# A hand-ordered attention and expert kernel: one key load moved behind the weights, two factor products and a weight conversion re-seated, four stores issued by ScalarE

## The chip, the cores and the metric

The kernel runs on one core of a Trainium2 chip. The metric is the device time of one execution in microseconds (us): a median of 152.86 us over three runs (152.83 to 153.1). Five engines share the work, each with its own instruction list that it works off strictly in order: TensorE (PE in the profile), VectorE (DVE), ScalarE (ACT), GpSimd (POOL) and SyncE (SP), which issues most of the transfers. A wait in one list holds everything behind it on that engine.

## The reference

Two stages follow each other. The first is attention with 4 batches, 8 heads, 768 tokens and head size 64. A query sees the 8 first ("global") keys and a window of 96 keys behind it, with a bias that falls with distance, a slope per head:

```
scores = scale * q @ k.T
keep = is_global | is_local          # first 8 keys, or 0 <= i-j < 96
scores = where(keep, scores + bias, -1e9)
a = exp(scores - max); a = a / (sum(a) + 1e-9)
attn = a @ v
```

The second takes the 3072 tokens of 512 numbers that result:

```
h = x @ w_in                          # 512 -> 1024
solu = h * softmax(h)
ln = (solu - mean) / sqrt(var + 1e-6) * g_ln
out = ln @ w_out                      # 1024 -> 512
```

## The kernel before

**Tiling.** Heads are worked on in pairs (4 pairs per batch). The scores of a pair are cut into two groups of key blocks (queries 0 to 383 need the first, the rest the second too). The second stage goes by 24 tiles of 128 tokens. Batch 0 is on the critical path at the start; from about 26 us on, the second stage of one batch is interleaved with the attention of the next.

**Attention, step by step.** A pair's k or q is loaded as fp32 (`x32_`, lines 477 and 484), converted to fp16 (`x16_`, helper lines 264 on ScalarE, 266 on VectorE, 268 on GpSimd), turned by six TensorE transposes into a bank of PSUM (line 741), and copied out of the bank as `kT` or `qT`. In the last batch the turn is a DMA transpose (776). TensorE forms the scores (878 and 892), ScalarE their exponential `eb` (900). In batches 1 to 3 the bias is not added but multiplied in afterwards, as a factor `fb` (909, "the factor product"): on VectorE in one instruction, on GpSimd in four pieces. TensorE then sums the weights (973, 982), spreads the logarithm of the sums (1028), ScalarE takes the reciprocal `rr` (1037), and TensorE multiplies by v in two halves (1072); between the halves VectorE copies one number out of the bank (`tick`, 1082), and the second half waits for it. VectorE makes the product `xT` (1097), which is the input of the second stage.

**Second stage.** First product with w_in (1133), exponential `ef` (1140), `uu` (1143), its squares (1150 or 1154), a turn of `uu` (by TensorE at 1169, or by DMA at 1159), the second product (1215), a scaling into `osb` (1226, 1229) and the store (1233). Before the second product can run, w_out is loaded, multiplied by g (644, 647, 651: "weighing"), its mean taken on TensorE (658) and subtracted by eight VectorE instructions (662: "the centring").

**What sets the order.** All steps are numbered while the program is written; nothing else decides their order than the table `ORDER`, a list of these numbers, from which the five instruction lists follow. `SLOTS` gives each step its buffers, among them the eight PSUM banks; `ENGS` gives the engine of a step that has a choice; `WARM` places matmuls without use among the first steps. Transfers issued by SyncE and ScalarE take turns over eight semaphores, so that each issue waits until the transfer eight before it has landed.

Of the kernel before, what the change touches and what calls it, by code (L numbers as in the profile page):

```python
# [60 lines left out]
"""  # L61
SLOTS = """
# [10 lines left out]
"""  # L73
ENGS = """
# [1206 lines left out]
```

## Time and profile before

| | |
|---|---|
| Median of three runs | 152.86 us |
| The profiled execution | 152.65 us, of it 150.9 us span of instructions |
| TensorE busy | 142.4 us (94%) |
| ScalarE / VectorE / GpSimd busy | 122.1 / 117.9 / 69.9 us |
| Granted TensorE clock | full in all 40 slices |
| DMA busy | 9 tenths or more in 30 of 40 slices |

The page gives each engine's busy time, the busy tenths in 40 slices and the chain of work that ended last, followed back from the end. The timeline lists instructions with their start in us from the span's start, their length, and in square brackets the idle time of the engine just before them with what ended it; neighbours of one form are merged into a row (x4 is four instructions, and the length is that from the first start to the last end). Instructions of an engine overlap by some 0.05 to 0.08 us when they follow each other without a hole. PEld is TensorE's loading of weights, which comes just ahead of the matmul.

### The profile page before, as it was taken

How to read it: one execution, taken by the hardware profiler on the slowest of the kernel's cores; microseconds unless marked ns; L12 is line 12 of the kernel's file. 1: busy time of each engine (PE TensorE's matmuls, PEld its weight loads, DVE VectorE, ACT ScalarE, POOL GpSimd, SP SyncE). 2: the span in 40 equal slices, each digit the busy share in tenths (PEclk: the TensorE clock that was granted, in tenths of full speed). 3: DMA queues.
4: the chain of work that ended last, by engine and by line, in shares of the span. 5: the costliest groups of instructions: out<-in, count | busy, mean ns of one | idle time of the engine just before them, and what ended most of it. 6: DMA issues, size and time to landing. Idle time of an engine off the chain costs nothing.

```text
span 150.9 us, 4802 instructions
## 1 busy us (share of the span) xinstructions
PE 142.4 (94%) x1870; PEld 76.7 (51%) x1870; DVE 117.9 (78%) x241; ACT 122.1 (81%) x209; POOL 69.9 (46%) x192
## 2 busy tenths in 40 slices
PE   5979799999998999999999999999999999999991
PEld 2536556466554566744454645444446644444450
DVE  6939897998999997989899966697785874898200
ACT  3949899899999789899997987978895776874641
POOL 6784447559899769735922240498130000110000
PEclk9999999999999999999999999999999999999999
DMA  4999999999999999999999999998999946488743
GB/s 140 367 307 342 300 382 337 362 337 401 309 295 182 247 323 220 240 216 250 241 160 235 260 161 260 162 221 159 223 212 260 216 125 128 81 245 208 231 152 139
DMA packets 76430, 36.35 MB, mean 241 GB/s; under 512 B 65456, under 2 KB 71928, under 8 KB 76408
## 3 DMA queue, kind: packets, MB, share of 16 engines
q1 hardware_dynamic: 76120, 35.54, 97.5%
q10 hardware_dynamic: 288, 0.52, 0.9%
q8 instruction: 14, 0.23, 0.6%
q14 instruction: 8, 0.07, 0.1%
HBM read 23.15 MB, written 6.29 MB: 195 GB/s over the span
## 4 chain that ended last, share of the span: by engine, by line
PE 72%; ACT 9%; DMA 7%; SPq 5%; DVE 4%; issue 1%; DVEq 0%; ACTq 0%
PE acc L1215 28%; PE acc L1133 23%; PE acc L1072 6%; DMA vt<-in_v_dram 4%; DMA x<-in_q_dram 3%; PE acc L892 3%; ACT eb L900 3%; PE acc L1028 3%; PE acc L973 2%; PE acc L741 2%; SPq L477 2%; ACT ef L1140 2%; DVE x L266 2%; PE acc L1062 1%; SPq L499 1%
## 5 line engine op out<-in xcount | busy, mean ns | idle before, releaser
L1215 PE MATMUL acc<-gw_out_sb,late 128*128 128x512 f16 (+1 forms) x200 | 44.3, 371 | 0.4 <-DMA vt<-in_v_dram 0.4
L1133 PE MATMUL acc<-w_in_sb,xT 128*128 128x512 f16 x192 | 44.7, 379 | 0.0
L1143 DVE SCALAR_TENSOR_TENSOR uu<-ef,acc 128x1024 f16<-128x1024 f16 x24 | 29.2, 1216 | 8.6 <-ACT ef L1140 8.4
L900 ACT ACTIVATE eb<-acc 128x896 f16<-128x896 f32 (+1 forms) x32 | 29.1, 955 | 1.5 <-PE acc L892 1.4
L1140 ACT ACTIVATE ef<-acc 128x1024 f16<-128x1024 f32 x24 | 24.7, 1030 | 6.5 <-PE acc L1133 6.5
L1215 PEld LDWEIGHTS <-late 128*128 128x128 f16 x200 | 18.9, 98 | 21.5 <-issue 1.3
L1133 PEld LDWEIGHTS <-xT 128*128 128x128 f16 x192 | 17.8, 98 | 21.4 <-issue 1.4
L268 POOL CAST x<-x 128x384 f16<-128x384 f32 (+1 forms) x32 | 17.9, 586 | 12.3 <-DMA x<-in_q_dram 6.2
L1097 DVE TENSOR_TENSOR xT<-acc,rr 128x384 f16<-128x384 f32 x32 | 16.3, 551 | 3.9 <-ACT rr L1037 1.5
L1072 PE MATMUL acc<-eb,v 64*64 64x160 f16 (+4 forms) x448 | 16.0, 221 | 0.6 <-DVE xT L1097 0.3
L1150 ACT ACTIVATE sqa<-uu 128x1024 f16<-128x1024 f16 x15 | 15.9, 1063 | 0.0
L909 POOL TENSOR_TENSOR eb<-eb,fb 128x240 f16<-128x240 f16 (+1 forms) x20 | 12.5, 656 | 6.1 <-ACT eb L900 6.1
L1072 PEld LDWEIGHTS <-v 64*64 64x64 f16 x448 | 12.9, 106 | 4.5 <-issue 3.4
L1037 ACT ACTIVATE rr<-acc 128x768 f32<-128x768 f32 x16 | 12.6, 811 | 2.8 <-PE acc L1028 1.9
L268 POOL CAST v<-v 128x384 f16<-128x384 f32 (+3 forms) x23 | 10.9, 492 | 7.2 <-DMA v<-in_v_dram 6.3
L909 DVE TENSOR_TENSOR eb<-eb,fb 128x896 f16<-128x896 f16 (+1 forms) x19 | 13.3, 727 | 1.1 <-ACT eb L900 1.1
L741 PE MATMUL acc<-ident,x 128*128 128x128 f16 x144 | 11.1, 220 | 1.5 <-ACT x L264 1.0
L892 PE MATMUL acc<-qT,kT 64*64 64x160 f16 (+2 forms) x384 | 11.8, 227 | 0.0
L1154 DVE SCALAR_TENSOR_TENSOR sqv<-uu 128x1024 f16<-128x1024 f16 x9 | 11.3, 1251 | 0.1
L741 PEld LDWEIGHTS <-x 128*128 128x128 f16 x144 | 8.5, 98 | 4.8 <-ACT x L264 1.4
L1226 ACT ACTIVATE x<-acc,rstd 128x512 f32<-128x512 f32 (+1 forms) x9 | 5.8, 640 | 6.2 <-PE acc L1215 6.2
L1062 PE MATMUL acc<-eg,vgz 64*64 64x384 f16 x64 | 10.7, 324 | 0.0
(120 smaller groups left out, 206.1 us busy)
## 6 DMA issues: line engine op xcount, KB each, us to landing
x<-in_q_dram SPq DMA_DIRECT2D x16, 384.0 KB, 5.8
x<-in_k_dram SPq DMA_DIRECT2D x16, 384.0 KB, 5.1
out_dram<-osb SPq DMA_DIRECT2D x12, 256.0 KB, 4.9
v<-in_v_dram SPq DMA_DIRECT2D x12, 192.0 KB, 4.5
out_dram<-x SPq DMA_DIRECT2D x9, 256.0 KB, 2.3
late<-in_moe_w_in_dram SPq DMA_DIRECT2D x4, 512.0 KB, 6.6
w_out<-in_moe_w_out_dram SPq DMA_DIRECT2D x4, 512.0 KB, 6.0
v<-in_v_dram SPq DMA_DIRECT2D x12, 160.0 KB, 4.7
```

The lines of the kernel that those rows point to most:

```text
L268: nc.gpsimd.tensor_copy(out=out, in_=in_)
L741: nc.tensor.transpose(out=pt[:, ts(j, P)], in_=a[:, j, ts(pp, P)], identity=ident)
L892: nc.tensor.matmul(out=sc[o : o + 64, par, col : col + n], lhsT=kk[r, BLK * c : BLK * c + BLK], rhs=qq[r, g0 : g0 + n], start=fresh, stop= ...
L900: ex["fn"] = (lambda ex=ex, qk=qk, gw=gw: nc.scalar.activation(out=eb[at(qk, "eb")][:, :, 0:gw], in_=big(qk)[:, :, 0:gw], func=AF.Exp, sca ...
L909: (nc.gpsimd if fx["at"] == "POOL" else nc.vector).tensor_tensor(out=e[:, :, y], in0=e[:, :, y], in1=fb[:, p, :, y], op=ALU.mult)
L1072: nc.tensor.matmul(out=o_[64 * h : 64 * h + 64, gl : gl + m], lhsT=vv[r, v_at(vi, h, c), pair, :], rhs=view(eb[at(e_own[b, gi, pair], "eb" ...
L1097: nc.vector.tensor_tensor(out=xT[at(xt_own[b], "xT")][:, p, q0:q1], in0=one(av, d)[:, 0:w], in1=rr[at(re, "rr")][:, d, 0:w], op=ALU.mult)
L1133: nc.tensor.matmul(out=ph()[:, ts(fh, 512)], lhsT=xT[at(xt_own[b], "xT")][:, j, ts(t % NA, P)], rhs=w_in_sb[:, j, ts(fh, 512)], start=((j, ...
L1140: ex["fn"] = lambda g1=g1, t=t, ph=ph: nc.scalar.activation(out=ef[at(g1, "ef")], in_=ph(), func=AF.Exp, accum_out=s0[:, t : t + 1])
L1143: u["fn"] = lambda u=u, g1=g1, t=t, ph=ph: nc.vector.scalar_tensor_tensor(out=uu[at(u, "uu")], in0=ef[at(g1, "ef")], scalar=USC, in1=ph(), ...
L1150: nc.scalar.activation(out=sqs_["ACT"], in_=uu[at(u, "uu")], func=AF.Square, scale=float(D_FF) ** 0.5, accum_out=s2[:, t : t + 1])
L1215: nc.tensor.matmul(out=one(g2)[:, 0:wd], lhsT=uT[at(el_o, "uT")][:, c, :], rhs=gw_out_sb[:, c, sl_], start=(c == 0), stop=(c == NFC - 1))
```

## The change

- The load of the k of pair 1 of the second batch (`x32_3`) stands behind the third and fourth quarter of w_in and the load of g on SyncE. Its turn on TensorE stands behind the first two tiles of the first product, and goes to bank 7 and not 2. ScalarE copies it out behind the second `ef`.
- One of the casts of w_in (second half of its first quarter) goes from ScalarE to GpSimd.
- The turn of the last q of batch 0 goes to bank 0 and not 4.
- The eight small memsets of `slr` go from GpSimd to VectorE.
- The factor product of the second group of pair 0, batch 1 (`eb9`), goes from VectorE to GpSimd; that of pair 1 (`eb10`) stays on VectorE but stands behind the centring.
- Four stores of tiles below 20 go from SyncE to ScalarE. Some GpSimd steps near 96 to 103 us change places.

```diff
 ORDER = """
-126 86 12 11 271 2 13 17 16 10 15 66 14 18 0 20 73 36 3 75 7 1 4 88 68 69 89 22 53 55 56 90 8 70 38 79 81
+126 271 2 52 86 12 11 18 66 13 73 0 36 3 53 17 20 7 16 38 10 15 14 1 79 4 88 28 68 115 22 60 75 117 69 89
...
 WARM = """
-25:0:16 30:2:4 37:3:2 48:5:3 118:7:4
+34:0:16 43:2:4 49:3:2 59:5:3 126:7:4
...
     def constants_slr():
         for h in range(H):
-            nc.gpsimd.memset(slr[:, h : h + 1], -slopes[h] * NL)
+            nc.vector.memset(slr[:, h : h + 1], -slopes[h] * NL)
...
-    slr_st = step("POOL", 270, -59000, [], constants_slr, name="c_slr")
+    slr_st = step("DVE", 560, -59000, [], constants_slr, name="c_slr")
...
-                        wd * 1.31, tg + 2500, [ou], eng=("SP",) if x < 20 else ("SP", "ACT"), name="store", iss=420)
+                        wd * 1.31, tg + 2500, [ou], eng=("SP", "ACT"), name="store", iss=420)
```

GpSimd's list between 21 and 35 us of the trace, as a difference (x32_3 is the moved k, x32_5 the q of pair 3, x32_0 and x32_1 the k of pairs 2 and 3, all of the second batch; kg holds the global keys):

```order
 L268 CAST v16_1_115<-v32_0_111 128x2x3x64
+L268 CAST w_in_sb_69<-late_154 128x512 x4
 L268 CAST x16_3_110<-x32_3_103 128x384 x2
-L268 CAST w_in_sb_69<-late_154 128x512 x3
-L523 TENSOR_TENSOR kg1_127<-kT1_117,hpick_84 128x16
 L268 CAST x16_2_109<-x32_4_104 128x384 x2
 L268 CAST x16_0_107<-x32_5_105 128x384 x2
+L909 TENSOR_TENSOR eb9_139<-eb9_139,fb_166 128x2x112 x4
 L647 TENSOR_TENSOR gw_out_sb_71<-w_out32_70,g32_72 128x256 x2
 L268 CAST x16_3_110<-x32_0_100 128x384 x2
+L523 TENSOR_TENSOR kg1_127<-kT1_117,hpick_84 128x16
 L268 CAST x16_2_109<-x32_1_101 128x384 x2
```

Four pieces of a factor product and one kg product now stand ahead of the conversion of x32_1, and four casts of w_in ahead of that of x32_3.

VectorE's list from 39 to 50 us of the trace, before:

```order
L909 TENSOR_TENSOR eb11_141<-eb11_141,fb_166 128x960
L909 TENSOR_TENSOR eb10_140<-eb10_140,fb_166 128x2x448
L1097 TENSOR_TENSOR xT0_98<-acc_158,rr1_147 128x384
L266 COPY late_154<-acc_158 128x1024
L1097 TENSOR_TENSOR xT0_98<-acc_158,rr1_147 128x384
L662 SCALAR_TENSOR_TENSOR gw_out_sb_71<-w_out32_70,g32_72,acc_158 128x512 x8
L1143 SCALAR_TENSOR_TENSOR uu3_153,sums3_92<-ef1_149,acc_158 128x1024
L266 COPY qT0_121<-acc_158 128x768
```

and in the changed kernel:

```order
L909 TENSOR_TENSOR eb11_141<-eb11_141,fb_166 128x960
L1097 TENSOR_TENSOR xT0_98<-acc_158,rr1_147 128x384
L266 COPY late_154<-acc_158 128x1024
L1097 TENSOR_TENSOR xT0_98<-acc_158,rr1_147 128x384
L662 SCALAR_TENSOR_TENSOR gw_out_sb_71<-w_out32_70,g32_72,acc_158 128x512 x8
L1143 SCALAR_TENSOR_TENSOR uu3_153,sums3_92<-ef1_149,acc_158 128x1024
L909 TENSOR_TENSOR eb10_140<-eb10_140,fb_166 128x2x448
L266 COPY qT0_121<-acc_158 128x768
```

The product of eb10 moved behind the eight centring instructions and one `uu`; the set of instructions in this stretch is the same.

## Rows read from the trace of the kernel before

**Rows 1.** The page: the chain that ended last, shares by engine.

```profile
PE 72%; ACT 9%; DMA 7%; SPq 5%; DVE 4%; issue 1%; DVEq 0%; ACTq 0%
```

**Rows 2.** The chain in order of time: start us, us, what.

```profile
48.17 1.89 PE acc L1215 x8
...
56.36 0.30 PE acc L1072 x5
```

**Rows 3.** Busy us by stretch: PE, PEld, DVE, ACT, POOL, clock, DMA share, GB/s.

```profile
38.95:56.20 17.25, 16.70 (x225) 8.81 (x222) 17.25 (x29) 15.71 (x28) 14.05 (x29) 1.00 1.09 264
...
57.00:147.80 90.80, 90.76 (x1050) 46.51 (x1047) 67.75 (x129) 71.61 (x128) 29.11 (x68) 1.00 0.97 202
```

**Rows 4.** Timeline of VectorE: start us, us, engine, instruction [idle before].

```profile
35.30 0.96 DVE L266 COPY kT<-acc 128x768 f16<-128x768 f16 x1
36.30 0.16 DVE L1082 COPY tick<-acc 128x1 f32<-128x1 f32 x1
...
37.19 1.02 DVE L1097 TENSOR_TENSOR xT<-acc,rr 128x384 f16<-128x384 f32 x2 [0.32 <-PE acc L892]
...
38.88 0.16 DVE L1082 COPY tick<-acc 128x1 f32<-128x1 f32 x1
...
56.16 0.14 DVE L1082 COPY tick<-acc 128x1 f32<-128x1 f32 x1
```

**Rows 5.** Timeline of TensorE and its weight loads around 34.5 us.

```profile
34.42 0.77 PE L741 MATMUL acc<-ident,x 128*128 128x128 f16 x6
...
34.85 0.17 PEld L741 LDWEIGHTS <-x 128*128 128x128 f16 x3 [0.26 <-POOL x L268]
```

**Rows 6.** Timeline of GpSimd, 27 to 35 us.

```profile
27.38 0.21 POOL L523 TENSOR_TENSOR kg<-kT,hpick 128x16 f16<-128x16 f16 x1 [1.13 <-ACT kT L264]
...
28.90 0.96 POOL L268 CAST x<-x 128x384 f16<-128x384 f32 x2 [0.41 <-DMA x<-in_q_dram]
31.66 1.18 POOL L647 TENSOR_TENSOR gw_out_sb<-w_out,g 128x256 f16<-128x256 f32 x2 [1.80 <-DMA w_out<-in_moe_w_out_dram]
32.78 2.01 POOL L268 CAST x<-x 128x384 f16<-128x384 f32 x4
```

**Rows 7.** Timeline of GpSimd: its factor products elsewhere.

```profile
96.54 2.31 POOL L909 TENSOR_TENSOR eb<-eb,fb 128x224 f16<-128x224 f16 x4 [5.89 <-ACT eb L900]
...
58.52 2.74 POOL L909 TENSOR_TENSOR eb<-eb,fb 128x240 f16<-128x240 f16 x4
...
41.66 4.81 POOL L909 TENSOR_TENSOR eb<-eb,fb 128x240 f16<-128x240 f16 x8
```

**Rows 8.** Timeline of VectorE: a factor product, and two conversions of q or k.

```profile
28.04 0.92 DVE L909 TENSOR_TENSOR eb<-eb,fb 128x896 f16<-128x896 f16 x1
...
30.26 0.56 DVE L266 CAST x<-x 128x768 f16<-128x768 f32 x1 [0.15 <-DMA x<-in_q_dram]
...
59.70 1.06 DVE L266 CAST x<-x 128x768 f16<-128x768 f32 x1
```

**Rows 9.** Timeline of ScalarE at 17.7 us and TensorE at 25.4 us.

```profile
17.74 0.58 ACT L959 ACTIVATE eg<-acc,gbias 128x384 f16<-128x384 f32 x1 [0.38 <-PE acc L946]
...
25.42 0.51 PE L741 MATMUL acc<-ident,x 128*128 128x128 f16 x6
25.77 0.60 PE L1133 MATMUL acc<-w_in_sb,xT 128*128 128x512 f16 x2
```

**Rows 10.** Timeline of VectorE and of GpSimd around 11 us.

```profile
11.01 0.72 DVE L266 CAST x<-x 128x768 f16<-128x768 f32 x1 [2.55 <-DMA x<-in_q_dram]
...
10.99 0.33 POOL L374 MEMSET slr<- 128x1 f32 x8
```

**Rows 11.** Timeline of ScalarE at 82.7 us, and a store it issues late.

```profile
82.68 0.81 ACT L1037 ACTIVATE rr<-acc 128x768 f32<-128x768 f32 x1 [0.77 <-PE acc L1028]
...
143.37 0.37 ACTq L1233 DMA_DIRECT2D out_dram<-x  x1
```

**Rows 12.** Timeline of TensorE at 48.2 us.

```profile
48.17 0.38 PE L1215 MATMUL acc<-gw_out_sb,late 128*128 128x512 f16 x1 [0.43 <-DMA vt<-in_v_dram]
```

82 rows, old and new, of tables (ENGS, ORDER, SLOTS) are left out of this document.

## The prediction, as put on record before the run

> **What bounds the kernel now.** I read the chain that ended last first, since it says where a gain would count. TensorE holds 72% of it [rows 1], and from 48 us on it is TensorE alone [rows 2]. The table by stretch says the same of the end: from 57 to 147.8 us TensorE is busy for 90.76 of 90.8 us [rows 3]. So whatever TensorE has lost or won by 57 us is lost or won at the end; nothing behind it can be hidden or recovered but a few tenths.
>
> What sets the time at 57 us? At 56.36 the second half of an attention product starts [rows 2], and the VectorE copy it waits for (`tick`) runs from 56.16 to 56.30 [rows 4]: 0.06 us from one to the other. TensorE waits for VectorE there. And VectorE is busy for 17.25 of the 17.25 us from 38.95 to 56.20 [rows 3]: one run of 29 instructions without a hole. The start of this run sets its end.
>
> Followed backwards, the run begins behind the tick at 38.88. That waits for an attention product, whose bank is freed by the `xT` products at 37.19, which wait for TensorE (0.32 idle); that work waits for the tick at 36.30; and this stands behind the copy of `kT` at 35.30 [rows 4]. The copy needs six transposes of k that start at 34.42 and stop halfway: the last three begin at 34.85, and what TensorE waited for is GpSimd's conversion [rows 5]. GpSimd converts in two pieces, and the second of this k ends at 34.79 (32.78 + 2.01) [rows 6]. So one conversion on GpSimd, of the k of pair 3 of batch 1, carries the time of the whole kernel through five engine hand-overs. GpSimd is the least busy engine of all, which is why the shares alone would mislead.
>
> **The change part by part.**
>
> *The factor product on GpSimd.* In the changed list it stands right behind the conversion of 28.90, which waited 0.41 for its load and ends at 29.86. GpSimd then was idle for 1.80 us until the weighing of w_out at 31.66 [rows 6]. Four pieces of the same shape took 2.31 [rows 7]. With the overlap of about 0.05 at each seam the weighing starts at 29.81 + 2.31 - 0.06 = 32.06 and not at 31.66: +0.40. All behind it is back to back: two weighing pieces, two conversion pieces, then the kg product of 0.21 (0.16 with its seam) that now stands between the two conversions: +0.16. The four conversion pieces took 2.01; two take 0.96, so four without a hole take 1.86, and 0.15 was a hole that the delay fills: -0.15. Sum so far +0.41.
>
> *What it meets there.* VectorE's conversion at 30.26 starts when its load lands (0.15 idle) and took 0.56 [rows 8]. It will now fall among the pieces. The trace has this very meeting: at 59.70 such a conversion took 1.06, and the four pieces around it 2.74, where eight undisturbed ones took 4.81, so four take 2.42 [rows 7, 8]. GpSimd lost 0.32 and VectorE 0.50. I add +0.32 to GpSimd. VectorE's 0.50 delays its own list to the same `kT` copy by no more than GpSimd's delay does, and stands beside it. The Trainium skill (SBUF — State Buffer, "Who interferes with whom") states that the two engines share a port pair which the first to start keeps for its whole instruction while the other fully blocks. By that rule GpSimd would lose up to the whole 0.56 of the conversion, and the total would be 0.97 in place of 0.73; the row of 59.70, where both lost, bears the rule out in kind and is smaller in size, and I use the row.
>
> So the second piece of the conversion ends at 34.79 + 0.73 = 35.52, the last three transposes, the copy, both ticks and VectorE's run follow by +0.73.
>
> *The product taken from VectorE at 28.04* (0.92, rows 8). Behind it VectorE waits for a load at 30.26 anyway, so it shortens nothing on the path. Worth 0; if that load were earlier, up to 0.85.
>
> *The product put behind the centring.* It leaves its place inside the run of 38.95 to 56.20 and enters it again at about 49: same instructions, same length of the run. The centring ends 0.85 earlier relative to the run, and TensorE's wait of 0.43 at 48.17 (put down to a transfer, in truth the end of the last centring instruction) goes [rows 12]. But TensorE then only waits longer for the tick that was at 56.16. Worth 0.
>
> *The bank, the cast, the k load.* With the other bank the turn at the end of batch 0 need not wait for an exponential; ScalarE's 0.38 idle at 17.74 goes, and with ScalarE in a run from there on, all up to 25 us is 0.38 earlier. The six transposes ahead of the first product took 25.42 to 25.77, so that starts another 0.35 earlier [rows 9]. That is 0.73 gained at 26 us, and I count it 0: the loads are paced by a DMA system that is busy throughout (share 1.09 in the stretch of rows 3), the conversion of 28.90 starts when its load lands [rows 6], the load has the same bytes in front of it as before, and from there the sum above runs. Bounds: 0.3 either way if its issue, which waits for another transfer's landing now, shifts the landing.
>
> *The `slr` memsets.* VectorE was idle for 2.55 ahead of 11.01, and eight memsets took 0.33 on GpSimd [rows 10]; three times that still fits. 0.
>
> *The four stores on ScalarE.* A store issued there took 0.37 of its queue [rows 11]. Two fall into the stretch ahead of 82.68, where ScalarE was idle for 0.77, the others into similar holes. 0; without that cover about 0.4, if one must wait for a transfer as GpSimd does for 0.41 at 28.90 [rows 6].
>
> Sum: the profiled execution took 152.65, of it 150.9 span. 152.65 + 0.73 = 153.38. The median of the runs is 0.21 above the profiled one, so in its terms 152.86 + 0.73 = 153.59, said as 153.6. Bounds of this case: 0.41 without the meeting and up to 0.97 + 0.3 = 1.27 with a full block and a late load, so 153.2 to 154.1.
>
> **Rivals.**
>
> *No change.* The lateness of the conversion is swallowed: the load behind 28.90 lands 0.4 to 0.7 earlier, or the pieces run quicker. For it: GpSimd has idled 0.41 there for a transfer, the v conversion of 11 us starts 0.33 earlier without the memsets, and SyncE's later issues follow. Against: transfers are busy throughout. The time stays at 152.9. Chance 0.22.
>
> *Faster.* The gain of 0.73 at 26 us comes through to the transposes at 34.42: their k is converted in time and VectorE's run starts earlier. That decides at one point: the end of the conversion must lie ahead of 34.79 and not behind it, so the loads have to come more than 0.73 earlier. Then the 0.26 at 34.85, 0.32 of VectorE's idle time at 37.19 and what TensorE lost around them go: 152.86 - 0.6 = 152.3. For it: the casts of w_in are ready sooner. Against: the same transfers. Chance 0.13.
>
> *Slower by more, elsewhere.* A store at the head of ScalarE's list waits for its turn among the eight semaphores at 82 us and holds `rr` behind it; `xT` and the next first product follow. Decides if the wait is over the hole of 0.77 less two issues of 0.37. Price 0.4 on top of the sum: 154.0. For it: TensorE has no slack there. Against: the transfers that these stores follow are long landed. Chance 0.08.
>
> **How the numbers follow.** The forecast has 0.57, no change 0.22, faster 0.13, the stores 0.08. A measurement of this kernel can tell 0.2%, 0.31 us, from no change. The forecast's own range begins at +0.41, so it lies on the slower side but for the odd case: slower 0.57 + 0.08 - 0.02 = 0.63, same 0.22 + 0.02 = 0.24, faster 0.13. The range 152.7 to 154.1 takes in no change and the upper bound; left out are most of the faster case and the tail of the stores, under 2 in 10.
>
> **What would show it.** Right: on GpSimd four pieces from about 29.8 that take 2.3 to 2.7 with a VectorE conversion of about 1.0 beside them; the weighing at 32.1 or later with no idle time ahead of it; the last three transposes at about 35.6 (34.85 before) with GpSimd named as what they waited for; the tick of 56.16 at about 56.9 while TensorE's wait at 48.17 is gone; and the same TensorE work from there to the end. Also the first product ahead of 25.1, with its gain used up in waits between 31 and 35.5. Wrong: the conversion of 28.90 starting earlier than 28.5, VectorE's run starting by another route than this k, or a TensorE wait of over 0.3 past 60.

## The result, and the profile after

The changed kernel takes 155.21 us (median of 6 runs, 153.97 to 157.01) against 153.0 of the kernel before on the same chip: ratio 1.0121, interval 1.0075 to 1.0167, or +1.85 us (1.15 to 2.55). Run again (e5 below): 1.0119 (1.0073 to 1.0165). It is slower, as forecast, but by two and a half times the 0.73 of the sum, and outside the range. The ratios here and below are of undisturbed executions, and the traces of e2 and e8, which were disturbed, aren't used.

The profiled execution took 155.23 against 152.65, +2.58; its span is 153.14 against 150.91, +2.23. GpSimd's list where the sum was made, from the timeline (start us, us, engine, instruction, idle time before it), answering [rows 6]:

```profile
26.25 0.61 POOL L268 CAST w_in_sb<-late 128x512 f16<-128x512 f32 x1 [1.68 <-DMA late<-in_moe_w_in_dram]
27.38 2.23 POOL L268 CAST x<-x 128x384 f16<-128x384 f32 x4 [0.52 <-PE acc L1133]
30.07 0.96 POOL L268 CAST x<-x 128x384 f16<-128x384 f32 x2 [0.45 <-DMA x<-in_q_dram]
30.99 2.62 POOL L909 TENSOR_TENSOR eb<-eb,fb 128x224 f16<-128x224 f16 x4
33.57 1.18 POOL L647 TENSOR_TENSOR gw_out_sb<-w_out,g 128x256 f16<-128x256 f32 x2
34.70 0.95 POOL L268 CAST x<-x 128x384 f16<-128x384 f32 x2
35.61 0.21 POOL L523 TENSOR_TENSOR kg<-kT,hpick 128x16 f16<-128x16 f16 x1
35.77 0.95 POOL L268 CAST x<-x 128x384 f16<-128x384 f32 x2
```

The product took 2.62, the undisturbed 2.31 of [rows 7] and the 0.31 of the meeting; the weighing behind it waits for nothing, the kg product stands between the two conversions. VectorE's conversion among the pieces took 0.74 (0.56 before [rows 8]), where about 1.0 was forecast. From the start of the q conversion to the end of the last k conversion it is 30.07 to 36.72, 6.65 us, against 28.90 to 34.80, 5.90: +0.75. But the q conversion itself starts at 30.07 and not at 28.90, because its load landed later: +1.17. Of the q loads on SyncE it is this one, by the semaphore that the conversion waits for; before and changed:

```profile
22.97 0.67 SPq L477 DMA_DIRECT2D x<-in_q_dram  x1
```

```profile
23.39 1.10 SPq L477 DMA_DIRECT2D x<-in_q_dram  x1
26.21 0.37 SPq L491 DMA_DIRECT2D v<-in_v_dram  x1
27.27 0.37 SPq L631 DMA_DIRECT2D w_out<-in_moe_w_out_dram  x1
```

VectorE behind it, the same view, answering [rows 4]:

```profile
37.22 0.96 DVE L266 COPY kT<-acc 128x768 f16<-128x768 f16 x1 [0.87 <-PE acc L741]
38.23 0.16 DVE L1082 COPY tick<-acc 128x1 f32<-128x1 f32 x1
39.11 1.02 DVE L1097 TENSOR_TENSOR xT<-acc,rr 128x384 f16<-128x384 f32 x2 [0.32 <-PE acc L892]
40.80 0.16 DVE L1082 COPY tick<-acc 128x1 f32<-128x1 f32 x1
40.87 1.21 DVE L651 TENSOR_SCALAR gw_out_sb<-w_out,g 128x512 f16<-128x512 f32 x2
42.01 0.95 DVE L909 TENSOR_TENSOR eb<-eb,fb 128x960 f16<-128x960 f16 x1
58.46 0.14 DVE L1082 COPY tick<-acc 128x1 f32<-128x1 f32 x1
```

Every hand-over of the forecast is there, 4.08 us from the end of the conversion to the tick at 40.80, as before (34.80 to 38.88). The run from there to the tick at 58.46 is 17.66 and was 17.28. Busy time by stretch (columns as in [rows 3]) shows it still without a hole, and TensorE full behind it:

```profile
40.87:58.50 17.63, 16.38 (x221) 8.46 (x219) 17.63 (x29) 15.52 (x27) 16.84 (x33) 1.00 1.19 265
59.50:150.00 90.50, 90.48 (x1044) 46.27 (x1035) 67.68 (x129) 71.56 (x127) 27.76 (x64) 1.00 0.99 198
```

GpSimd is busy for 16.84 of that stretch and was for 14.05 [rows 3]. The account of this execution's span is +1.17 for the load, +0.75 for GpSimd's list, +0.38 for VectorE's run, -0.07 behind it: 2.23. The other 0.35 lies outside the span: time less span is 2.09 here and was 1.74. That is no chance of one execution. All six executions of the changed kernel have 2.05 to 2.13, and in the kernel before it is 1.66 to 1.79 in every execution of every set. So some 0.36 of the 1.85 comes ahead of the first or behind the last instruction, where no trace shows what it is.

TensorE's timeline has two waits in the run, of which the forecast knew one:

```profile
49.81 1.89 PE L1215 MATMUL acc<-gw_out_sb,late 128*128 128x512 f16 x8 [0.41 <-DVE gw_out_sb L662]
54.48 0.22 PE L878 MATMUL acc<-bw,identb 64*64 64x64 f16 x2 [0.77 <-DVE uu L1143]
```

The first stood at 48.17 [rows 12] and should have gone. The second is new: the scores of a pair wait for a bank that VectorE's second `uu` frees, and between the centring and that `uu` the product of eb10 now stands.

### The profile page after: what moved, and what is told of

Its sections match the earlier page's. It is cut to its first block, busy times and chain, and to the rows that moved or that the text cites. A ratio compares the mean times of both kernels' runs of the same rounds, so it can differ in the third digit from the quotient of the medians.

```text
span 153.1 us, 4806 instructions
## 1 busy us (share of the span) xinstructions
PE 143.7 (94%) x1870; PEld 76.7 (50%) x1870; DVE 118.1 (77%) x248; ACT 121.6 (79%) x208; POOL 74.0 (48%) x189
## 4 chain that ended last, share of the span: by engine, by line
PE 62%; DVE 7%; issue 1%; ACT 0%
PE acc L1215 26%; PE acc L1133 21%; PE acc L1072 5%; DVE gw_out_sb L662 3%; PE acc L892 2%; PE acc L973 2%; PE acc L1028 2%; PE acc L741 1%; PE acc L1062 1%; DVE uu L1143 1%; DVE xT L1097 1%; PE acc L946 1%; PE acc L1169 1%; DVE qT L266 1%; PE acc L982 1%
## 5 line engine op out<-in xcount | busy, mean ns | idle before, releaser
L909 POOL TENSOR_TENSOR eb<-eb,fb 128x240 f16<-128x240 f16 (+1 forms) x24 | 16.9, 739 | 1.2 <-ACT eb L900 1.2
L268 POOL CAST v<-v 128x384 f16<-128x384 f32 (+3 forms) x23 | 10.1, 459 | 8.4 <-DMA v<-in_v_dram 6.2
L1242 PE MATMUL acc<-busy 128*128 128x512 f16 x29 | 9.5, 481 | 1.5 <-DVE busy L552 1.5
```

Of the source, the lines that this page charges most:

```text
L268: nc.gpsimd.tensor_copy(out=out, in_=in_)
L909: (nc.gpsimd if fx["at"] == "POOL" else nc.vector).tensor_tensor(out=e[:, :, y], in0=e[:, :, y], in1=fb[:, p, :, y], op=ALU.mult)
```

## The experiments

Every one is made from the kernel before or from the changed one. Ratios are to the kernel before on the same chip, with a 95% interval. The edits are shown as differences of an engine's instruction list, cut to the lines that differ.

**Four that take the change apart.** I first read the late load as the cause: three quarters of w_in stand together on SyncE, and a v load waited there until 26.21, behind the landing of the last of them. That reading had the wrong transfer: the q load whose conversion starts at 30.07 was issued at 23.39, ahead of this wait.

e1, the product alone:

```diff
 VectorE
-L909 TENSOR_TENSOR eb9_139<-eb9_139,fb_166 128x2x448
 GpSimd, behind the conversion of x32_5
+L909 TENSOR_TENSOR eb9_139<-eb9_139,fb_166 128x2x112 x4
```

> The kernel before, and of the change only the factor product of eb9 on GpSimd. The load theory (most of the +2.2 us comes from the loads, which the last quarter of w_in holds up since the k load moved): the conversion that began at 28.90 begins there again, the weighing at 31.66 begins at 32.1 to 32.4, the second piece of the last k conversion ends at 35.3 to 35.6 and not 34.79, and the time is 153.0 + 0.7 = 153.7 us (153.3 to 153.9). The product theory (the product alone makes the whole loss, the late load belongs to that one execution): 154.8 to 155.3. No change would say that the weighing's w_out load hides the product.

Measured: 1.0036 (1.0006 to 1.0066), +0.55 us. GpSimd and then VectorE:

```profile
28.48 0.22 POOL L523 TENSOR_TENSOR kg<-kT,hpick 128x16 f16<-128x16 f16 x1 [0.86 <-ACT kT L264]
28.64 1.99 POOL L268 CAST x<-x 128x384 f16<-128x384 f32 x4
30.59 2.62 POOL L909 TENSOR_TENSOR eb<-eb,fb 128x224 f16<-128x224 f16 x4
33.17 1.18 POOL L647 TENSOR_TENSOR gw_out_sb<-w_out,g 128x256 f16<-128x256 f32 x2
34.30 1.85 POOL L268 CAST x<-x 128x384 f16<-128x384 f32 x4
```

```profile
40.30 1.21 DVE L651 TENSOR_SCALAR gw_out_sb<-w_out,g 128x512 f16<-128x512 f32 x2
41.44 1.93 DVE L909 TENSOR_TENSOR eb<-eb,fb 128x960 f16<-128x960 f16 x2
```

The same product, the same 2.62. The q conversion starts late here too, at 29.67 inside the first row of conversions, and for two causes at once: its load landed at 29.55, by its semaphore, and GpSimd, late since the kg product waited for ScalarE's copy of `kT`, was ready for it only at 29.59. On VectorE the pair of weighings took 0.96 before and 1.21 here, the two products 1.49 and 1.93. Before:

```profile
38.95 0.96 DVE L651 TENSOR_SCALAR gw_out_sb<-w_out,g 128x512 f16<-128x512 f32 x2
39.84 1.49 DVE L909 TENSOR_TENSOR eb<-eb,fb 128x960 f16<-128x960 f16 x2
```

```profile
39.95 1.74 POOL L268 CAST x<-x 128x384 f16<-128x384 f32 x2 [0.71 <-DMA x<-in_k_dram]
```

GpSimd idled 0.71 ahead of 39.95 in the kernel before and works through now, so the two engines meet a second time. The run is 17.79.

e2, everything but the product (e1's edit, undone in the changed kernel):

> The changed kernel with the factor product of eb9 back on VectorE, in its place before the change. Load theory: the conversion still begins at about 30.1 (28.90 before the change), the weighing behind it waits for w_out, whose load was issued at 27.27 instead of 25.60, and starts at 32.5 to 33.3; the last k conversion ends 0.9 to 1.6 later than 34.79, and the time is 153.0 + 0.9 to 1.6 plus 0.4 for the product of eb10, 154.2 to 155.0. Product theory: the whole loss goes, 152.8 to 153.2.

Measured: 0.9986 (0.9955 to 1.0017). All other parts together cost nothing that shows without the product. The load theory said 154.2 to 155.0; as a cause without the product it is out. The time outside the span is that of the kernel before again, 1.67 to 1.76.

e3, the changed kernel with the moved k back, and e4, the moved k alone on the kernel before. SyncE's list in e4 (e3 the other way round; conversion, turn, copy and kg product move with it):

```diff
 L621 DMA late_154<-in_moe_w_in_dram 128x1024
-L477 DMA x32_3_103<-in_k_dram 128x2x384
 L621 DMA late_154<-in_moe_w_in_dram 128x1024 x2
 L584 DMA g8_73<-in_moe_g_ln_dram 8x128
+L477 DMA x32_3_103<-in_k_dram 128x2x384
```

> The changed kernel with the k of pair 1 of batch 1 back in its old places: its load between the second and third quarter of w_in, g between the third and fourth, its conversion, turn (bank 2), copy and kg product as before. Load theory: SyncE's v load goes at about 24.2 again instead of 26.2, the conversion that began at 30.07 begins at about 28.9, and with the product still on GpSimd the time is 155.2 - 1.2 = 154.0 (153.7 to 154.3). Product theory: no better than the changed kernel, 155.0 to 155.4.

> The kernel before, and of the change only the moved k of pair 1 of batch 1 (load behind w_in and g, conversion behind the casts of w_in, turn in bank 7 behind two tiles of the first product, copy behind the second ef, kg product later). Load theory: SyncE stops in front of a v load until the last quarter of w_in lands (25.5 to 26.2), the conversion that began at 28.90 begins at 29.8 to 30.2, the weighing waits for a w_out that is issued 1.2 to 1.7 later, and the time is 153.9 to 154.6. Product theory: 152.8 to 153.2.

Measured: e3 1.0087 (1.0052 to 1.0122), between its two theories, e4 0.9989 (0.9952 to 1.0026). In e4's trace the q conversion begins at 29.11, with the k load in its new place; so the new place doesn't by itself make that load 1.17 late. The load's time differs from execution to execution.

**Four on the chain.** e5 is the changed kernel again, e6 has the product behind the last k conversion, e7 the product of eb10 ahead of the centring again. e8 is a try at a faster kernel.

```diff
 e6, GpSimd
-L909 TENSOR_TENSOR eb9_139<-eb9_139,fb_166 128x2x112 x4
 L647 TENSOR_TENSOR gw_out_sb_71<-w_out32_70,g32_72 128x256 x2
...
 L268 CAST x16_2_109<-x32_1_101 128x384 x2
+L909 TENSOR_TENSOR eb9_139<-eb9_139,fb_166 128x2x112 x4
```

> The changed kernel itself, once more, beside the others of this set. Two theories stand. Chain theory: the factor product fills the 1.80 us that GpSimd waited ahead of the weighing of w_out; behind it GpSimd has no hole, the last k conversion ends 3.5 + 3.1 us behind the start of the conversion that waits for the q load, whenever that lands, and VectorE's run behind it is 0.4 to 0.7 longer, since GpSimd now works beside its first instructions, where it idled 0.71 before. Bank theory: the product of eb10, now behind the centring, delays the uu that frees the bank of the next scores, and TensorE's stall of 1.08 us ahead of 54.48 is the loss. Both say 154.5 to 155.3 us here, ratio 1.008 to 1.015.

> The changed kernel with the factor product of eb9 still on GpSimd, but behind the two pieces of the last k conversion of batch 1 instead of ahead of the weighing of w_out. Chain theory: GpSimd waits for w_out again ahead of the weighing, the last k conversion ends at 34.8 to 35.3 and the tick that was at 38.88 is at 38.9 to 39.4; the meeting in VectorE's run stays (0.4 to 0.7), so 153.2 to 153.9 us, ratio 1.001 to 1.005. Bank theory: as the changed kernel, 1.008 to 1.015, with the stall ahead of the scores still about 1 us.

> The changed kernel with the factor product of eb10 back ahead of the xT product and the centring. Bank theory: TensorE's stall ahead of the scores goes back from 1.08 to under 0.3 us, and the time falls by 0.7 to 1.0, ratio 1.002 to 1.006. Chain theory: the run of VectorE has the same instructions either way, the uu that frees the bank ends as late as before, and the time stays within 0.3 us of the changed kernel, 1.008 to 1.015.

Measured: e5 1.0119 (1.0073 to 1.0165), e6 1.0287 (1.0229 to 1.0344), e7 1.0167 (1.0115 to 1.0220). e5's profiled execution is its fastest, 153.99, and has the load on time:

```profile
29.06 0.96 POOL L268 CAST x<-x 128x384 f16<-128x384 f32 x2 [0.54 <-DMA x<-in_q_dram]
29.98 2.63 POOL L909 TENSOR_TENSOR eb<-eb,fb 128x224 f16<-128x224 f16 x4
32.57 1.19 POOL L647 TENSOR_TENSOR gw_out_sb<-w_out,g 128x256 f16<-128x256 f32 x2
```

Its last k conversion ends at 35.72, 6.66 behind 29.06, its run is 17.37, and its span 151.93, 1.02 above before. Inside the span that is close to the forecast; its time is 1.34 above before, with the 0.35 outside the span. The other five executions of e5 took 154.24 to 156.06.

e6 went against my chain theory. The k conversion was early, but TensorE then waited for the v conversions that stand behind the product on GpSimd:

```profile
37.67 0.26 PE L1072 MATMUL acc<-eb,v 64*64 64x160 f16 x2 [1.44 <-POOL v L268]
```

GpSimd's list has no room for 2.3 us there either. The wait isn't the whole price of e6: behind it the granted clock was at its lower level, 1.2 GHz, from 38 to 41 and again from 45 to 48 us (0.50 in both stretches). e7 rules out the new wait for the bank: that wait is gone in its trace and the time isn't better, though this trace has waits near 110 and 117 us that the changed kernel's lacks. Its two products at 41.91 take 1.93 as in e1 and the run is 17.95; behind the centring eb10 does less harm.

e8, two VectorE instructions moved back in the kernel before:

```diff
-L909 TENSOR_TENSOR eb_140<-eb_140,fb 128x2x448
 L1097 TENSOR_TENSOR xT_98<-acc,rr_147 128x384
...
 L1143 SCALAR_TENSOR_TENSOR uu_150,sums_92<-ef_148,acc 128x1024
+L909 TENSOR_TENSOR eb_140<-eb_140,fb 128x2x448
...
+L1082 COPY tick<-acc 128x1
 L1229 TENSOR_SCALAR osb_156<-acc,rstd 128x512
-L1082 COPY tick<-acc 128x1
```

> The kernel before with two VectorE instructions moved back: the product of eb10 (0.75 us) from ahead of the xT product at 41.25 to behind the uu that ends at 51.87, and the scaling into osb (0.74) from ahead of the tick at 56.16 to behind it. If VectorE's run sets TensorE's times, the centring, the uu and the tick all come 0.66 to 0.75 earlier; TensorE can only take up its own waits of 0.43 at 48.17 and 0.2 at 56.36, so the time falls by 0.3 to 0.6, to 152.4 to 152.7, ratio 0.996 to 0.998. If the sums of pair 1 then wait for the product, or the bank that osb frees is missing, it comes out at 1.000 or above.

Measured: 1.0030 (0.9997 to 1.0063). No gain.

**Is the hole a buffer?** e9 and e10 put two memsets into GpSimd's list ahead of the q conversion, in the kernel before and in the changed one; e11 adds the cast of w_in to e1; e12 is the changed kernel with the q load earlier:

```diff
 e9, e10, GpSimd
+L1249 MEMSET pad 128x512 x2
 L268 CAST x_0_107<-x_5_105 128x384 x2
 e12, SyncE
+L477 DMA x_5_105<-in_q_dram 128x2x384
 L491 DMA v_0_111<-in_v_dram 128x3x64
 L491 DMA v_1_112<-in_v_dram 128x2x64
-L477 DMA x_5_105<-in_q_dram 128x2x384
```

> The kernel before with two GpSimd memsets of 128x512 (about 1 us together, estimated from memsets of 128x128 at 0.2 and 128x256 at 0.32) between the conversions of the q of pair 2 and pair 3 of batch 1, that is ahead of the conversion that began at 28.90. They write a tile that nobody reads. Hole theory: GpSimd's waits behind it (0.41 and 1.80) take the 1 us up, the weighing begins at 31.7 as before, and the time is unchanged, ratio 0.998 to 1.002. If GpSimd's conversions there were already on the path, it is 0.5 to 1.0 us slower, ratio 1.003 to 1.007.

> The changed kernel with the same two GpSimd memsets at the same place. Hole theory: the product has filled the hole, so of the 1 us only the wait of about 0.5 for the q load is left to take it up, and the last k conversion and with it the end come 0.5 to 1.0 later: ratio to the kernel before 1.015 to 1.019, against 1.012 without the memsets. If the loss is not GpSimd's list, the ratio stays at 1.012.

> The kernel before with the factor product of eb9 on GpSimd and also the fourth cast of w_in on GpSimd (bank 0 for the turned q with it). The product alone gave 1.0036, the whole change without the k load 1.0087. If the difference is the 0.61 us that the cast adds to GpSimd's list ahead of the filled hole, this is 1.006 to 1.010, with GpSimd's conversions from 24 us on without idle time. If the cast is taken up by GpSimd's waits for loads, it is 1.002 to 1.005, and the difference lies elsewhere.

> The changed kernel with the load of the q of pair 3, whose conversion stands just ahead of the product, issued before two v loads that stood ahead of it (about 1.4 to 2 us earlier on SyncE). Hole theory: GpSimd's wait of 0.45 to 0.55 for this load goes, the conversion starts right behind the one ahead, and the end comes 0.4 to 0.6 earlier (more in executions where the load lands late): ratio 1.006 to 1.010. If the time of this load isn't on the path, 1.012; if the two v loads are, 1.012 or more.

Measured: e9 0.9997 (0.9971 to 1.0023), e10 1.0116 (1.0079 to 1.0154), e11 1.0048 (1.0022 to 1.0073), e12 1.0070 (1.0037 to 1.0104). e9:

```profile
28.59 1.11 POOL L1249 MEMSET pad<- 128x512 f16 x2
29.65 0.95 POOL L268 CAST x<-x 128x384 f16<-128x384 f32 x2
31.96 1.18 POOL L648 TENSOR_TENSOR gw_out_sb<-w_out,g 128x256 f16<-128x256 f32 x2 [1.36 <-DVE qT L266]
```

In the kernel before the q conversion can start at 29.65 at no cost: 1.36 of the hole are left. This delays GpSimd and no transfer. A late load is another case, since w_out, which ends the hole, is issued behind the q load. In e10 it starts at 30.16 with no hole behind it, and the time is that of the changed kernel, where I expected 0.5 to 1.0 more. That fits if the changed kernel's q load is usually not there before 30 (30.07 in its first trace, 29.98 in e7's, but 29.06 in e5's); it isn't shown, and e3, e17 and e18, the changed kernel but for one part, have 29.12 to 29.33. In e12, with the load two places earlier, the wait of 0.45 is gone

```profile
26.25 3.53 POOL L268 CAST x<-x 128x384 f16<-128x384 f32 x6 [0.56 <-DMA x<-in_k_dram]
29.74 2.62 POOL L909 TENSOR_TENSOR eb<-eb,fb 128x224 f16<-128x224 f16 x4
```

and the loss is 0.7 us smaller than e10's on the same chip (1.0070 against 1.0116, but the intervals overlap, and 0.17 of it is time outside the span, 1.92 in the mean against 2.09). The cast, in e11, adds nothing that shows.

**What does the product need beside it?** e13 is e1 with e4's edit, e15 is e1 with eb10 behind the centring, e14 is e1 with the four stores on ScalarE, the `slr` memsets and the later GpSimd order; e17 and e18 undo, in the changed kernel, the stores, and the memsets with the GpSimd order.

```diff
 e17: SyncE at its old places (e14: the other way round)
+L1233 DMA out_0_dram<-osb2_157 128x512
 ScalarE
-L1233 DMA out_0_dram<-osb2_157 128x512
 (and three more)
```

> The kernel before with two parts of the change: the factor product of eb9 on GpSimd and the moved k of pair 1 of batch 1 (load, conversion, turn, copy, kg product). The product alone gave 1.0036, the k alone 0.9989. If the two add up, 1.003 to 1.005. If the moved k makes the q load behind it land later (about 30 instead of 29) and the filled hole lets this through, 1.008 to 1.013, as the whole change.

> The kernel before with the product of eb9 on GpSimd, the four stores on ScalarE, the order of GpSimd's steps near 100 us and the slr memsets on VectorE as in the change. If these others are worth nothing: 1.003 to 1.005, as the product alone. If the stores on ScalarE or the GpSimd order hold up the last batch's loads (a wait of TensorE for a v conversion of 0.4 to 1.0 us near 116 us showed in some executions): 1.008 to 1.012.

> The kernel before with the product of eb9 on GpSimd and that of eb10 behind the centring on VectorE, nothing else. If the two add up to what the traces show of VectorE's run (same instructions, less of it beside GpSimd's eight pieces): 1.000 to 1.004. If eb10's place costs TensorE more by the late scores: 1.006 to 1.012.

> The changed kernel with the four stores back on SyncE at their old places, all else as changed. The product together with the k load (1.0059), with the cast (1.0048) or with the product of eb10 (1.003) stays near the product alone (1.0036), while all kernels with the stores on ScalarE and the product came out at 1.007 to 1.020. If the stores make the difference: 1.003 to 1.007. If it is the order of GpSimd's steps near 100 us or the slr memsets, or the sum of all: 1.010 to 1.014.

> The changed kernel with the order of GpSimd's steps near 100 us and the slr memsets as before the change, the stores still on ScalarE. If the GpSimd order or the memsets make the difference: 1.003 to 1.007. If the stores do, or the sum of all: 1.010 to 1.014.

Measured: e13 1.0059 (1.0024 to 1.0094), e14 1.0198 (1.0143 to 1.0254), e15 1.0030 (0.9990 to 1.0071), e17 1.0089 (1.0054 to 1.0124), e18 1.0069 (1.0032 to 1.0105). No single partner makes the loss. The traces of e11 and e14 are weak witnesses: their granted clock was at its lower level, 1.2 GHz, from 11.2 to 14.6 us (0.50 between 12 and 14). e14's excess over the changed kernel has its own cause, which the trace shows on ScalarE and then TensorE:

```profile
95.33 0.21 ACT L1198 ACTIVATE rstd<-vb 128x3 f32<-128x3 f32 x1
97.03 0.34 ACTq L1233 DMA_DIRECT2D out_dram<-osb  x1
97.49 0.69 ACT L1226 ACTIVATE osb<-acc,rstd 128x512 f32<-128x512 f32 x1 [1.95 <-PE acc L892]
```

```profile
98.23 1.02 PE L1133 MATMUL acc<-w_in_sb,xT 128*128 128x512 f16 x4 [0.93 <-ACT osb L1226]
```

The fourth store waits at the head of ScalarE's list from 95.54 to 97.03; the chain names the transfer that holds it, a DMA transpose of `uu` that is under way from 89.69 to 97.03. The `osb` behind the store frees a bank that TensorE needs. In the changed kernel the same store went off at 95.02, right behind the `rstd` of 95.01: there its turn among the semaphores falls behind another store, landed at 92.42, and not behind the transpose.

In e17 and e18 the load was on time (29.12, 29.22), and TensorE lost time at another place, here e18:

```profile
107.98 0.46 PE L892 MATMUL acc<-qT,kT 64*64 64x160 f16 x14 [0.30 <-DMA qT<-x]
115.80 0.25 PE L1072 MATMUL acc<-eb,v 64*64 64x160 f16 x1 [0.32 <-POOL v L268]
```

The last batch's transposed q and its v come late. These two waits are 0.62 of the 1.13 by which the way from the second tick to the end grows, 94.75 to 95.88. e7 has them too:

```profile
117.61 0.25 PE L1072 MATMUL acc<-eb,v 64*64 64x160 f16 x1 [0.60 <-POOL v L268]
```

e16 was to test the chain by shortening it:

```diff
 SyncE: the k loads of pairs 2 and 3 ahead of a v, a q and the first w_out load
+L477 DMA x32_0_100<-in_k_dram 128x2x384
+L477 DMA x32_1_101<-in_k_dram 128x2x384
...
-L477 DMA x32_0_100<-in_k_dram 128x2x384
-L477 DMA x32_1_101<-in_k_dram 128x2x384
 GpSimd: the weighing behind their conversions
```

> Made from what the traces show, not a part of the change: in the kernel before, the two k loads of pairs 2 and 3 of batch 1 are issued ahead of a v load, a q load and the first w_out load (about 2 us earlier), and GpSimd converts them ahead of the first weighing of w_out, for which it waited 1.80 us. If this k conversion sets the time, as the chain says, it ends 1 to 2 us earlier than 34.79, TensorE's waits of 0.26 at 34.85 and 0.32 on VectorE at 37.19 go, and the time falls by 0.3 to 0.8: ratio 0.995 to 0.998. If the weighing, the q load or the v load that are now later are the next limit, 1.000 or above.

Measured: 1.0132 (1.0077 to 1.0188). The last k conversion ended at 33.45, 1.35 earlier, but the q load that gave way made TensorE wait:

```profile
34.43 0.51 PE L741 MATMUL acc<-ident,x 128*128 128x128 f16 x6 [1.40 <-DVE x L266]
```

No version beat the kernel before.

## Why the prediction was wrong

The account of each trace, by the steps of the forecast: start of the q conversion on GpSimd, from there to the end of the last k conversion, VectorE's run from tick to tick, from the second tick to the end of the span, and the time outside the span. (In e6 and e16 the steps stand in another order.)

| | time | q conv. starts | to end of k conv. | run | behind it | outside |
|---|---|---|---|---|---|---|
| before | 152.65 | 28.90 | 5.90 | 17.28 | 94.75 | 1.74 |
| e4, k alone | 152.63 | 29.11 | 5.85 | 17.00 | 94.87 | 1.72 |
| e9, memsets | 152.78 | 29.65 | 5.45 | 17.13 | 94.75 | 1.72 |
| e1, product alone | 154.57 | 29.67 | 6.48 | 17.79 | 94.84 | 1.71 |
| e15, and eb10 | 153.43 | 29.07 | 6.48 | 17.24 | 94.84 | 1.72 |
| e13, and k | 154.10 | 28.99 | 6.69 | 17.79 | 94.84 | 1.71 |
| e11, and cast | 155.60 | 29.99 | 6.82 | 16.54 | 96.31 | 1.73 |
| e14, and stores | 156.16 | 30.18 | 6.51 | 17.78 | 95.90 | 1.71 |
| changed | 155.23 | 30.07 | 6.65 | 17.66 | 94.68 | 2.09 |
| e5, changed again | 153.99 | 29.06 | 6.66 | 17.37 | 94.75 | 2.06 |
| e3, k back | 153.90 | 29.33 | 6.49 | 17.26 | 94.76 | 1.98 |
| e7, eb10 back | 156.88 | 29.98 | 6.65 | 17.95 | 96.15 | 2.08 |
| e10, memsets | 155.51 | 30.16 | 6.64 | 17.24 | 95.30 | 2.09 |
| e12, load early | 155.41 | 28.82 | 6.65 | 17.56 | 96.28 | 1.98 |
| e17, stores back | 155.68 | 29.12 | 6.69 | 17.79 | 95.90 | 2.09 |
| e18, GpSimd order back | 154.78 | 29.22 | 6.65 | 17.24 | 95.88 | 1.71 |

*What bounds it: right.* In all sixteen rows the way from the end of the last k conversion to the first tick is 4.08 us, but for e12 (4.12) and e11 (4.21).

*The factor product on GpSimd and what it meets: right, 0.73 forecast, 0.75 measured.* Without the kg product between the conversions it is 0.58 (e1, e15), so the kg product is some 0.17, where the sum gave it 0.16. The row of 59.70 was the right measure of the meeting: the product took 2.62 here and 2.31 + 0.32 were forecast. A full block (the rival total of 0.97) didn't show: GpSimd lost 0.31 and VectorE's conversion 0.18 (0.50 at 59.70).

*The step that failed: the bank, the cast, the k load, counted 0 with bounds of 0.3.* The sum took the start of the q conversion from one execution, 28.90, and let the load's landing move by 0.3 at most. In the profiled execution it started at 30.07: 1.17 of the 2.58. Of this 0.42 is the later issue, 23.39 against 22.97, the shift that the bound was for. The other 0.75 is the load itself: 6.68 from issue to conversion against 5.93, which the sum held fixed. Wherever else in the table the conversion waited for it, this took 5.64 to 5.96, and 6.80 in e7. In e5, the same kernel, it took 5.79 and the conversion started at 29.06, so the lateness belongs to the execution as far as is known; that the change makes it oftener isn't shown. The moved k isn't needed for it: e1 and e14 don't have it, and in their traces the same load took 6.82 and 7.11 from issue to landing, by its semaphore (6.56 in the changed kernel's, 5.81 before).

That the filled hole lets such a lateness through, where the hole would have taken it up, is argued and not shown. In the changed kernel's trace w_out, which ends the hole, was issued at 27.27 (25.60 before) and landed at 32.50 (31.52), by its semaphore. So without the product the weighing would have started some 0.98 later too (an estimate from these two landings): most of the 1.17 would have come in this execution either way. e9 shows the hole's worth only against a delay of GpSimd itself.

*A term that the sum doesn't have: the time outside the span, 0.35 in the profiled execution.* The forecast added its 0.73 to the whole time and so held this part fixed. It is 2.02 to 2.13 in every execution of the changed kernel, e5, e6, e7, e10 and e17, and 1.66 to 1.79 in every one of the kernel before, e1, e2, e4, e8, e9, e11, e13, e15, e16 and e18; in e3, e12 and e14 it goes from 1.70 to 2.08. So it goes when the product is back on VectorE (e2), and when the `slr` memsets and the GpSimd order are back (e18); the cause stays open.

*The product put behind the centring, counted 0 as "same instructions, same length of the run": wrong by 0.38 in the profiled execution.* The list is the same, its length isn't: GpSimd, late, works beside VectorE's first instructions. 0.25 fall on the weighing pair (0.96 to 1.21) and 0.2 on each product there. With eb10 ahead of the centring it is 0.5 to 0.67 (e1, e13, e14, e7; e11's shorter run begins behind a tick that waited for TensorE), behind it 0 to 0.5. So that part of the change is a small gain by the traces, though the intervals of e7 and e5 overlap. TensorE's wait of 48.17 didn't go (0.41 at 49.81): the centring starts 3.61 behind the first tick and 3.90 before, 0.29 earlier and not 0.85.

*"Nothing behind it can be hidden or recovered but a few tenths": right for the changed kernel's trace (94.68), wrong as a rule.* In e7, e11, e12, e17 and e18 it is another 1.1 to 1.6 behind the second tick, with TensorE waiting for the last batch's loads. The traces without the product in the table lack this, but they are three.

*The `slr` memsets, 0: right inside the span.* The eight took 0.17 ahead of an idle 2.46:

```profile
9.21 0.17 DVE L374 MEMSET slr<- 128x1 f32 x8
11.84 0.76 DVE L266 CAST x<-x 128x768 f16<-128x768 f32 x1 [2.46 <-DMA x<-in_q_dram]
```

*The stores, 0: right in the changed kernel's trace.* The rival that a store waits at the head of ScalarE's list was real in e14, at 97 us instead of 82, and cost TensorE 0.93.

*The other rivals.* No change and faster both needed the lateness to be swallowed or overtaken ahead of the k conversion. The first product starts at 26.00 in the changed kernel's trace (25.77 before) and at 25.51 in e5, so of the 0.73 that was to be won there 0.26 came in one trace and nothing in the other.

What stays open: the product alone or with one partner costs 0.46 to 0.9 us (e15, whose interval takes in 0, e1, e11, e13), the whole change 1.8, and undoing the k, the stores or the GpSimd order takes 0.5 to 0.8 off each time. Every trace with the whole change has the 0.75 on GpSimd's list, and every execution the 0.36 outside the span, which is also near half of what e18 takes off. The rest, some 0.7 of the 1.85, is a longer run, late loads and late last-batch loads in changing shares; whether the whole change has them oftener isn't settled, and one trace per kernel can't count them.

## What to carry to other kernels

Idle time of a side engine ahead of the chain that sets the end isn't free room. Work put there costs at least what is left over after the hole. What the hole still takes up can be tested by delaying the engine, as e9 does, but that says nothing of a late load: look at which transfer ends the hole, and whether it is late together with the first. Price a load by several executions and not by one. When a side engine becomes late as a whole, look also at what it used to idle beside: there the shared instructions get slower. And compare time less span before and after: a part of a loss can lie where no instruction is.

## What the runs showed of the hardware

A meeting of GpSimd and VectorE had a steady price: the four pieces beside one conversion took 2.62 to 2.66 in every trace with the product there (2.31 undisturbed), two weighings of w_out on VectorE 1.21 beside GpSimd and 0.96 alone, two factor products 1.93 and 1.49. Two GpSimd memsets of 128x512 fp16 took 1.11 us. One load of q, the same in each kernel, took 5.64 to 6.80 us from issue to the conversion that waited for it. The issue of one DMA transpose held SyncE for 1.25 us in places and for 4.52 at 89.83 in the changed kernel's trace.

```profile
89.83 4.52 SPq L1159 DMA_TRANSPOSE late<-uu  x1
99.92 1.25 SPq L1159 DMA_TRANSPOSE late<-uu  x1
```
